# A sixth tile of the first MLP product let into PSUM during the second inverse stage, and another order for the first token tile

## Chip, cores, metric

One core of a Trainium2 chip. The metric is the device time of one execution in microseconds (us); runs of one kernel mostly agree within 0.3%. TensorE does the matmuls; DVE is VectorE, ACT is ScalarE; PSUM is the memory of eight banks into which TensorE writes. The kernel before takes 133.91 us (median of 4, 133.81 to 134.03).

## The reference, cut to what matters

```python
x = A_x                                   # (1, 2048, 512), bf16
h = x + irfft2(rfft2(layernorm(x)) * W)   # spectral mixing
n = layernorm(layernorm(h))
u = gelu(einsum("bsd,sf->bdf", n, w1) + b1)      # first MLP product, over tokens: 2048 -> 1376
y = einsum("bdf,fs->bds", u, w2) + b2            # second MLP product: 1376 -> 2048
out = h + y.transpose(0, 2, 1)
```

The MLP mixes tokens. So the first product needs every token: its 11 output tiles of 128 features (the last has 96) each accumulate over 16 token tiles.

## The kernel before

The kernel records operations with their tiles, and a small list scheduler written in Python fixes, before anything runs, each engine's order and each PSUM bank. On the chip every engine goes through its list in order; semaphores hold an instruction until what it needs is there. A *unit* is one use of a bank; the unit's class has a limit of how many may be open at once, and a unit that is not `early` opens only when all of its inputs are scheduled.

The names of the prediction stand for these operations, for each token tile n:

```python
for s2 in range(NS2):                       # 16 token tiles
    unit = PsumUnit("g2", 1)
    for par in (1, 0):
        for pq in range(2):
            mm(f"g2_{s2}_{par}{pq}", ...)   # "g2": 4 matmuls, 256 columns
    act(f"eo_{s2}", EO[:, s2, :], ...)      # "eo": PSUM -> bf16, frees g2's bank
    unit = PsumUnit("g3", 1)
    mm(f"g3_{s2}", ...)                     # "g3": 1 matmul, 512 columns
    dve(f"tl_{s2}", ...)                    # "tl", "th": the two halves of TT
    dve(f"th_{s2}", ...)
    dve(f"h_{s2}", ...)                     # "h": the residual stream H, frees g3's bank
    act(f"q_{s2}", ...Square...accum=V2)    # "q": sum of squares
    act(f"r2_{s2}", ...)                    # "r": inverse root
    dve(f"hh_{s2}", ...)                    # "hh": normalised token tile HH
    for t in range(5):
        mm1(t, s2)                          # "mm1 t/n": 512 columns, one per open tile
# ... cut ...
for t in range(5, NFT):
    for s2 in range(NS2):
        mm1(t, s2)                          # the other six tiles
# ... gelu of each tile, then the second product: 16 x 11 matmuls, 16 x "fin", 16 stores
```

Of the eight banks five are kept by mm1 tiles 0 to 4 late in this stage. The rest serve g2 and g3.

## Time and profile before

| | before |
|---|---|
| time, median | 133.91 us |
| span of the profiled run | 132.2 us |
| first g2 matmul starts | 39.84 us |
| last matmul ends | 128.86 us |
| TensorE issue idle between these two, holes over 0.025 us | 2.26 us |

The last row is counted from the starts of TensorE's matmuls; a *hole* is what a start comes later than the spacing of two matmuls allows. The prediction shows how, with the lines that carry it.

### The profile page before, as it was taken

How to read it: one execution, taken by the hardware profiler on the slowest of the kernel's cores; microseconds unless marked ns; L12 is line 12 of the kernel's file. 1: busy time of each engine (PE TensorE's matmuls, PEld its weight loads, DVE VectorE, ACT ScalarE, POOL GpSimd, SP SyncE). 2: the span in 40 equal slices, each digit the busy share in tenths (PEclk: the TensorE clock that was granted, in tenths of full speed). 3: DMA queues.
4: the chain of work that ended last, by engine and by line, in shares of the span. 5: the costliest groups of instructions: out<-in, count | busy, mean ns of one | idle time of the engine just before them, and what ended most of it. 6: DMA issues, size and time to landing. Idle time of an engine off the chain costs nothing.

```text
span 132.2 us, 2004 instructions
## 1 busy us (share of the span) xinstructions
PE 123.3 (93%) x773; PEld 73.2 (55%) x773; DVE 70.5 (53%) x133; ACT 62.7 (47%) x144; POOL 10.7 (8%) x30
## 2 busy tenths in 40 slices
PE   6799989999979799999989999999999999999990
PEld 2145656878757455444334444456666666666650
DVE  0599978999973999999950000000332422423322
ACT  4299966789867999966699222222000000000000
POOL 0089900003000000000000000000000000000000
PEclk9999999999999999999999999999999999999998
DMA  3999999999999999980000000000112112121121
GB/s 110 340 401 388 303 291 295 297 215 332 394 418 416 410 413 413 386 208 31 0 0 0 0 0 0 0 5 0 40 40 79 40 40 79 45 75 44 40 79 40
DMA packets 16920, 22.16 MB, mean 168 GB/s; under 512 B 2736, under 2 KB 12720, under 8 KB 16912
## 3 DMA queue, kind: packets, MB, share of 16 engines
q1 hardware_dynamic: 16624, 21.52, 48.6%
q10 hardware_dynamic: 288, 0.52, 1.4%
q8 instruction: 6, 0.10, 0.3%
q14 instruction: 2, 0.02, 0.0%
HBM read 19.95 MB, written 2.10 MB: 167 GB/s over the span
## 4 chain that ended last, share of the span: by engine, by line
PE 60%; ACT 16%; DVE 16%; DMA 3%; issue 3%
PE ps L553 60%; ACT JK L571 5%; ACT Y L571 4%; DVE H L903 4%; DVE V L828 3%; DMA X<-in_A_x_dram 3%; ACT EO L571 3%; DVE HH L908 2%; ACT rs L571 2%; DVE TT L894 2%; DVE TT L896 2%; ACT r L571 2%; ACT FS L571 1%; DVE Y L744 1%; ACT PQ L571 1%
## 5 line engine op out<-in xcount | busy, mean ns | idle before, releaser
L553 PE MATMUL ps<-HH,W 128*128 128x512 bf16 (+1 forms) x176 | 41.0, 379 | 1.3 <-DVE HH L908 1.1
L553 PE MATMUL ps<-GT,W 128*128 128x512 bf16 (+1 forms) x176 | 38.2, 379 | 0.0
L933 DVE SCALAR_TENSOR_TENSOR OUT<-ps,B2f,H 128x512 bf16<-128x512 f32 x16 | 12.0, 750 | 48.7 <-PE ps L553 48.7
L553 PEld LDWEIGHTS ps<-GT,W 128*128 128x128 bf16 (+1 forms) x176 | 25.5, 145 | 12.6
L553 PEld LDWEIGHTS ps<-HH,W 128*128 128x128 bf16 (+1 forms) x176 | 17.1, 100 | 22.1 <-DVE HH L908 2.2
L828 DVE TENSOR_TENSOR V<-ps,W 128x2048 bf16<-128x2048 f32 (+1 forms) x8 | 15.7, 2017 | 0.4 <-PE ps L553 0.2
L571 ACT ACTIVATE GT<-ps,B1f 128x512 bf16<-128x512 f32 (+1 forms) x11 | 7.1, 688 | 14.6 <-PE ps L553 14.6
L571 ACT ACTIVATE JK<-H,nm 128x512 bf16<-128x512 bf16 x16 | 11.6, 726 | 3.4 <-DVE H L903 3.2
L682 DVE BATCH_NORM_STATS2 st<-X 128x6 f32<-128x512 bf16 x15 | 9.8, 665 | 3.6 <-DMA X<-in_A_x_dram 3.6
L903 DVE TENSOR_TENSOR H<-ps,TT 128x512 bf16<-128x512 f32 x16 | 10.9, 681 | 0.0
L571 ACT ACTIVATE PQ<-ps 128x512 bf16<-128x512 f32 (+1 forms) x16 | 9.1, 591 | 3.7 <-PE ps L553 3.6
L553 PE MATMUL ps<-EM,V 128*128 128x128 bf16 x128 | 9.6, 220 | 0.4 <-ACT PQ L571 0.3
L571 ACT ACTIVATE EO<-ps 128x512 bf16<-128x512 f32 x16 | 9.3, 600 | 0.9 <-PE ps L553 0.9
L648 PE MATMUL ps<-ZT 128*128 128x512 bf16 x21 | 7.6, 481 | 2.1 <-DVE ZT L591 1.2
L553 PE MATMUL ps<-FS,X 128*128 128x256 bf16 x64 | 8.6, 274 | 0.8 <-ACT FS L571 0.5
L571 ACT ACTIVATE CS<-ps 128x512 bf16<-128x512 f32 (+1 forms) x16 | 8.4, 577 | 1.6 <-PE ps L553 1.6
L553 PEld LDWEIGHTS ps<-EM,V 128*128 128x128 bf16 x128 | 7.8, 98 | 2.5 <-issue 1.3
L553 PE MATMUL ps<-EM,PQ 128*128 128x256 bf16 x64 | 8.6, 273 | 0.5 <-ACT PQ L571 0.5
L553 PE MATMUL ps<-EM,Y 128*128 128x256 bf16 x64 | 8.6, 273 | 0.4 <-DVE Y L744 0.4
L571 ACT ACTIVATE Y<-ps 128x512 bf16<-128x512 f32 (+1 forms) x15 | 7.9, 566 | 0.2 <-PE ps L553 0.2
L660 POOL TENSOR_SCALAR FS<-FP,rs 128x256 bf16<-128x256 bf16 x8 | 7.4, 937 | 6.7 <-ACT rs L571 6.4
L894 DVE TENSOR_TENSOR TT<-ps,X 128x256 f32<-128x256 f32 x16 | 6.7, 416 | 2.1 <-PE ps L553 2.1
(38 smaller groups left out, 77.9 us busy)
## 6 DMA issues: line engine op xcount, KB each, us to landing
W<-in_B_w_dram SPq DMA_DIRECT2D x8, 688.0 KB, 9.6
W<-in_B_w_dram SPq DMA_DIRECT2D x10, 512.0 KB, 17.0
out_dram<-OUT SPq DMA_DIRECT2D x16, 128.0 KB, 1.7
W<-in_A_w_r_dram SPq DMA_DIRECT2D x4, 257.0 KB, 5.2
W<-in_A_w_i_dram SPq DMA_DIRECT2D x4, 257.0 KB, 5.7
X<-in_A_x_dram SPq DMA_DIRECT2D x4, 256.0 KB, 5.0
X<-in_A_x_dram SPq DMA_DIRECT2D x2, 512.0 KB, 6.6
W<-in_A_w_r_dram SPq DMA_DIRECT2D x4, 192.8 KB, 4.5
```

What stands on the lines that cost most here:

```text
L553: return K.op(name, "pe", lambda eng, bank: eng.matmul(outf(bank), lhsT, rhs, start=start, stop=stop), ins=ins or [lhsT, rhs], occ=occ, la ...
L571: return eng.activation(dst, s, func, **kw)
L648: return K.op(name, "pe", lambda eng, bank: eng.matmul(ps[:, bank, :], ZT[:, 0:NP], ZT[:, :], start=True, stop=True), ins=[ZT[:, :]], occ= ...
L660: dve(f"fs_{i}", lambda eng, bank: eng.tensor_scalar(FS[:, i, :, :], FP[:, i, :, :], rs, None, op0=ALU.mult), [FP[:, i, :, :], rs], [FS[:, ...
L682: dve(f"bn_{i}", lambda eng, bank, i=i, x=x: eng.bn_stats(ST[:, i, 0:6], x), [x], [ST[:, i, 0:6]], 512, prio=25)
L744: dve(name, lambda eng, bank: eng.tensor_copy(dst, src(bank)), [], [dst], n, unit=unit, prio=28, last=last)
L828: return eng.tensor_tensor(vout, s, win, ALU.mult)
L894: dve(f"tl_{s2}", lambda eng, bank, tt=tt, xl=xl: eng.tensor_tensor(tt[:, 0, :], ps[:, bank, 256:512], xl, ALU.add), [xl], [tt[:, 0, :]], ...
L896: dve(f"th_{s2}", lambda eng, bank, tt=tt, xh=xh: eng.tensor_tensor(tt[:, 1, :], xh, ps[:, bank, 256:512], ALU.subtract), [xh], [tt[:, 1, ...
L903: return eng.tensor_tensor(hs.rearrange("p (h d) -> p h d", h=2), e, tt[:, :, :], ALU.add)
L908: dve(f"hh_{s2}", lambda eng, bank, s2=s2, hs=hs: eng.tensor_scalar(HH[:, s2, :], hs, NM[:, s2:s2 + 1], R2[:, s2:s2 + 1], op0=ALU.add, op1 ...
L933: dve(f"fin{s2}", lambda eng, bank, dst=dst, bia=bia, hs=hs: eng.scalar_tensor_tensor(dst, ps[:, bank, :], bia, hs, op0=ALU.add, op1=ALU.add),
```

## The change

It means to fill TensorE's idle time in the second inverse stage. Three things are meant: tile 5 and tile 6 of mm1 may take a bank as soon as one is free; DVE and ACT finish token 0 ahead of the next tokens, so that mm1 can begin sooner; and g2 of tokens 0 to 7 has a limit of its own, so that g2 of later tokens may open beside it.

```diff
-    "dve": """... fs_13 fs_14 fs_15 ys_12 ys_14""",
+    "dve": """... fs_13 fs_14 fs_15 ys_12 ys_14
+        tl_0 th_0 h_0 tl_1 th_1 h_1 hh_0""",
-    "act": """... ys_11 ys_13 yh_150 yh_151""",
+    "act": """... ys_11 ys_13 yh_150 yh_151
+        eo_0 eo_1 eo_2 eo_3 eo_4 q_0 r2_0 eo_5""",
+MM1B_FROM = {5: 54000.0, 6: 62000.0}
-    K = Builder(nc, {..., "g2": 2, "g3": 2, "mm1": 5, "mm1b": 6, "mm2": 8})
+    K = Builder(nc, {..., "g2a": 2, "g2": 2, "g3": 2, "mm1": 5, "mm1b": 6, "mm2": 8})
-            w1units[t] = PsumUnit("mm1" if t < 5 else "mm1b", 1, early=t < 5)
+            w1units[t] = PsumUnit("mm1" if t < 5 else "mm1b", 1, early=t < 7)
         mm(f"mm1_{t}_{s2}", ...,
-           s2 == 0, s2 == NS2 - 1, s2 == 0, 2 if t < 5 else 1, 512)
+           s2 == 0, s2 == NS2 - 1, s2 == 0, 2 if t < 5 else 1 if t < 6 else 0.5, 512, nb=MM1B_FROM.get(t, 0.0))
     for s2 in range(NS2):
-        unit = PsumUnit("g2", 1)
+        unit = PsumUnit("g2a" if s2 < 8 else "g2", 1)
```

(`mm` hands `nb` on as an earliest start, in ns of the scheduler's own clock.) No operation is added or taken away.

More of the change, by code (lines that the diff above doesn't have):

```diff
@@ L500 @@
     "dve": """bn_0 ag_0 bn_1 ag_1 bn_2 bn_4 ag_2 bn_5 ag_4 bn_6 ag_5 bn_7 ag_6 bn_8 ag_7 bn_9 ag_8 bn_10 ag_9 bn_11 ag_10 bn_12 ag_11
-        fs_9 ag_12 bn_13 fs_11 ag_13 bn_14 bn_15 ag_14 ag_15 fs_13 fs_14 fs_15 ys_12 ys_14""",
+        fs_9 ag_12 bn_13 fs_11 ag_13 bn_14 bn_15 ag_14 ag_15 fs_13 fs_14 fs_15 ys_12 ys_14
+        tl_0 th_0 h_0 tl_1 th_1 h_1 hh_0""",
     "act": """rs_0 fs_0 rs_1 s1_3 s2_3 rs_2 rs_3 fs_3 rs_4 ys_0 rs_5 ys_1 ys_3 rs_6 ys_2 fs_7 rs_8 ys_4 ys_5 rs_9 ys_7 rs_11 ys_6 ys_8
-        rs_13 ys_9 ys_10 rs_14 ys_11 ys_13 yh_150 yh_151""",
+        rs_13 ys_9 ys_10 rs_14 ys_11 ys_13 yh_150 yh_151
+        eo_0 eo_1 eo_2 eo_3 eo_4 q_0 r2_0 eo_5""",
     "pool": """fs_1 bv_3 fs_2 fs_4 fs_5 fs_6 fs_8 fs_10 fs_12""",
@@ L520, in build_kernel @@
     es.__enter__()
-    K = Builder(nc, {"f1": 7, "f2": 2, "x": 2, "g1": 2, "g2": 2, "g3": 2, "mm1": 5, "mm1b": 6, "mm2": 8})
+    K = Builder(nc, {"f1": 7, "f2": 2, "x": 2, "g1": 2, "g2a": 2, "g2": 2, "g3": 2, "mm1": 5, "mm1b": 6, "mm2": 8})
     K.forced = {e: FRONT[e].split() for e in ("dve", "act", "pool")}
@@ L545, in dma, with mm @@
                     rate=rate, occ=1000.0 if stream == "pool" else 640.0 if rate < DMA_RATE else 460.0, not_before=not_before, stall=stall)
-    def mm(name, outf, lhsT, rhs, unit, start, stop, first, prio, n, ins=None, half=False, after=()):
+    def mm(name, outf, lhsT, rhs, unit, start, stop, first, prio, n, ins=None, half=False, after=(), nb=0.0):
         occ = n / 2.4 + 3.0
@@ L553, in mm @@
         return K.op(name, "pe", lambda eng, bank: eng.matmul(outf(bank), lhsT, rhs, start=start, stop=stop),
-                    ins=ins or [lhsT, rhs], occ=occ, lat=n / 2.4 + 220.0, unit=unit, pw=True, first=first, prio=prio, after=after)
+                    ins=ins or [lhsT, rhs], occ=occ, lat=n / 2.4 + 220.0, unit=unit, pw=True, first=first, prio=prio, after=after, not_before=nb)
     def act(name, dst, src, func, n, ins=(), outs=None, unit=None, prio=0, last=True, psum=True, bias=None, scale=None, accum=None):
```

## The prediction

> **Names.** The second stage runs, for each of 16 token tiles n: four 256-column matmuls PQ to PSUM ("g2"), an ACT copy to EO ("eo"), one 512-column matmul ("g3"), three DVE ops (two halves of TT, called tl and th, then H, called h), on ACT the sum of squares (written to JK, "q") and its inverse root ("r"), and on DVE the normalised HH ("hh"). Each hh n releases one matmul of 512 columns per open tile t of the first MLP product ("mm1 t/n", 11 tiles). After that come the rest of mm1, the gelus, and 176 matmuls of the second product.
>
> **What bounds the kernel now.** I read the chain in order of time first. Its end:
> ```profile
> 66.30 0.34 DVE TT L896
> 66.64 0.02 issue
> 66.66 0.69 DVE H L903
> 67.35 0.33 DVE HH L908
> 67.68 0.05 issue
> 67.73 61.15 PE ps L553 x282
> 128.88 0.03 issue
> 128.90 0.75 DVE OUT L933
> ```
> From 67.73 us to 128.88 TensorE issues 282 matmuls back to back. 282 is 176 + 176 less the 70 mm1 matmuls done by then. There is no hole in them, so before that only two things can shorten the run: less TensorE work, or less TensorE idle time. The change removes no matmul. So the question is how much TensorE idles before 67.73 us, and how much of that stays. Before 39.84 us, where g2 begins, both programs have the same instructions in the same order.
>
> I measure idle time at TensorE's issue and not from its busy share, because the records overlap:
> ```profile
> 55.59 2.32 PE L553 MATMUL ps<-HH,W 128*128 128x512 bf16 x10
> ```
> Ten matmuls take 2.32 us, with 0.38 for the last one: (2.32 - 0.38)/9 = 0.216 us each, and likewise 0.109 for 256 columns (13 in 1.59 us). Then I took the TensorE timeline, start by start, and counted what each start comes later than the one before plus 0.216 or 0.109. The largest hole, and one of the late ones:
> ```profile
> 44.64 0.38 PE L553 MATMUL ps<-EO,IF 128*128 128x512 bf16 x1
> 45.88 0.38 PE L553 MATMUL ps<-HH,W 128*128 128x512 bf16 x1 [0.86 <-DVE HH L908]
> ...
> 64.23 1.87 PE L553 MATMUL ps<-HH,W 128*128 128x512 bf16 x7
> 66.35 2.84 PE L553 MATMUL ps<-HH,W 128*128 128x512 bf16 x11 [0.26 <-DVE HH L908]
> ```
> The first is 45.88 - 44.64 - 0.22 = 1.02 us of lost issue. All seven holes: 1.02 ahead of mm1 0/0 (waits for hh 0), 0.19 ahead of 0/1 (hh 1), 0.08 and 0.06 ahead of g3 5 and 8 (eo), 0.20, 0.42 and 0.29 ahead of 0/12, 0/13 and 0/14 (their hh). Sum 2.26 us. That is all that the change can win: 1.7% of 133.87.
>
> Why the holes: DVE. By windows,
> ```profile
> 50.00:55.00 5.00, 5.00 (x33) 2.73 (x31) 4.84 (x13) 5.00 (x15) 0.00 (x0) 1.00 1.02 415
> 55.00:60.00 5.00, 5.00 (x25) 2.29 (x24) 4.98 (x13) 3.53 (x10) 0.00 (x0) 1.00 0.86 223
> 60.00:65.00 5.00, 4.96 (x24) 2.10 (x23) 5.00 (x14) 3.54 (x10) 0.00 (x0) 1.00 0.05 14
> ```
> (columns: stretch, length, then busy PE, weight loads, DVE, ACT, POOL, clock, DMA share, GB/s) DVE is full. Spaced start to start in its timeline, tl and th take 0.33 each, h 0.60, hh 0.33: 1.59 us a token. TensorE needs 5 x 0.216 + 0.216 (g3) = 1.30. So TensorE catches up with DVE and from token 12 on waits for each hh.
>
> **What the Trainium skill says.** "TensorE: Matmul & The Clock Gate", section "Back-to-back issue gap", gives N/2.4 + 2.5 ns for a warm isolated matmul, 216 ns at 512 columns: the trace agrees with 0.216. The same section has about 131 ns for streams with weight loads; this trace, which has one load per matmul, doesn't show that. "Perfetto Trace Analysis", section "Identifying the Most-Contended Engine", warns that matmul busy time is no good measure of headroom: agreed, the windows say 5.00 of 5.00 where smaller holes sit between starts. "PSUM — Partial Sum Buffer", section "The four PSUM rules", has one matmul output in one of 8 banks, so a tile that is open holds a bank: here five tiles leave three banks to g3. "VectorE: DVE Perf Modes", section "The DRAIN you can't avoid", says that a Vector op reading what the one just before wrote still needs a semaphore; th then h directly takes 0.45 us start to start here (66.21 to 66.66), against 0.33 with an op between.
>
> **The change, part by part.** It adds and removes nothing; it moves. I took the new order on each engine with its waits and walked it with the spacings of the trace before: ACT eo to eo 0.49, eo to q 0.48, q to eo 0.71, eo to r 0.47, r to next 0.19, q to r direct 0.85; a released op starts 0.03 to 0.05 after the record it waits for, mm1 0.06 after hh (0.15 where it also waits for a load).
>
> (1) *First tile ahead.* h 0 now follows th 0 directly: 42.03 + 0.45 = 42.48, not 42.69. eo 5 no longer precedes q 0, which starts 0.48 after eo 4's 42.72: 43.20 instead of 43.81. Then eo 6 at 43.91, r 0 at 44.38, ended 44.67, hh 0 at 44.71 to 45.12, mm1 0/0 at 45.27 (was 45.88). In front of it TensorE now has g2 9 as well (up to 45.08), since tokens 8 and up have their own limit of two open g2 banks. The hole of 1.02 becomes 0.19.
>
> (2) *A new wait.* mm1 0/0, 1/0, 2/0 go at 45.27, 45.49, 45.71. Next stands g3 4, in the bank that g2 7 used, so it waits for eo 7. ACT: r 0 44.38, eo 5 44.57, q 1 45.05, eo 7 45.76 to 46.36; g3 4 at 46.41, where 45.92 was possible: 0.49 lost. This is the greatest loss that I find in the new order. It displaces the holes of 0.19 and 0.08 of before.
>
> (3) *Tokens 1 to 11.* On from there: mm1 0/1 at 47.29 and g2 11 at 48.36 start without a wait; mm1 0/2 waits for hh 2 (r 2 ends 48.37, hh 2 48.41 to 48.82), 0.07 lost; g2 13 waits for h 5, 0.03 lost. After it, eo, h and hh are each ready before TensorE comes to them (mm1 0/5 at 55.21 with hh 5 ended 53.45; 0/9 at 60.18 with hh 9 ended 59.88; 0/10 at 61.91 with hh 10 at 61.47).
>
> (4) *Tile 5 as filler.* h 11 frees its bank at 61.1, and ten matmuls of tile 5 stand between there and mm1 0/14: 2.16 us that ran after 67.73 before. The late waits against them: mm1 0/12 at 65.15 with hh 12 ended 64.95 (plus 0.15: just in time), 0/13 at 66.88 with 66.68, 0/14 at 68.39 with 68.06, 0/15 at 69.69 with 69.36. So 0.20 + 0.42 + 0.29 = 0.91 goes. Tile 6, though let in, stands wholly behind tile 5's last, so it fills nothing. DVE ends its last hh 0.4 us later than before (69.36 against 68.97), which costs nothing as long as filler covers it.
>
> (5) *Loads.* The last part of the first weights lands at 46.3 us, before any use in either order; the second weights by 62.1. No transfer is moved.
>
> Sum: idle after 0.19 + 0.49 + 0.07 + 0.03 = 0.78 us against 2.26; gain 1.48. Everything from mm1 0/15 on keeps its work and, but for bank numbers, its order. 133.87 - 1.48 = 132.39 us, 1.1% less.
>
> **Rivals.** (a) *DVE stays the bound and takes the gain back.* For it: DVE full for 10 us, and it ends later by my walk. Then some holes of 0.91 reappear at 0/12 to 0/15, where my slack is 0.05 to 0.3 us; with half of them back, 132.8; with nothing gained, 133.9. Against it: filler needs no hh that isn't there, and DVE needs only the last hh 1.3 us after TensorE has 0/14. (b) *All holes close:* 131.6. It needs g3 4 not to wait; ACT's order says it will. (c) *The wait on eo 7 is dearer.* ACT is full until 55 us and orders eo 5 behind r 0, so everything behind it is tight; if q 1 or eo 7 slips by 0.5 us, 132.9. (d) *Slower:* a sixth tile leaves two banks to g3, so a late h delays g3, then DVE (I find one such: tl 14 waits 0.3 us for g3 14). To lose over 1.5 us it would have to happen at every token; the order puts it in the last four only.
>
> **Range and chances.** The three runs before lie within 0.22 us. My walk's error is the sum of some forty small spacings on ACT and the slack at 0/12; I give 0.5 us either way, the lower end short of all holes closed. 131.9 to 132.9. Over 2% faster needs 131.2, below the floor of 131.6, so only an effect that I don't see: 3%. Over 2% slower would need new waits of 4 us: 1%.
>
> **What would show it.** In the profile after: mm1 0/0 near 45.3 us; a TensorE hole near 46 us released by ACT's EO, about 0.5 us; no hole after 52 us; the unbroken run to the end counting more than 282 matmuls, and starting earlier. Wrong would be: holes on HH after 60 us (rival a), or the same start of g3 4 but a hole near 1 us (rival c).

## The result, and the profile after

132.43 us (median of 4, 132.34 to 132.51) against 133.91. The ratio is 0.9889, with a 95% interval of 0.9872 to 0.9906. Ratios here are the mean time of one kernel's fast runs over that of the other's fast runs of the same rounds, so not quite the ratio of the medians. That is 1.1% faster, 1.48 us by the medians.

The first trace of the changed kernel holds 763 of its 773 matmul records (and all 773 weight loads), so its chain looks broken where nothing waits. Its end, piece by piece in order of time (start us, length us, what):

```profile
46.30 7.90 PE ps L556 x47
54.20 0.05 issue
54.26 10.74 PE ps L556 x49
65.00 0.05 issue
65.05 10.74 PE ps L556 x49
```

Each break takes the length of one matmul, 0.216 us from start to start in excess, and the next comes 49 records on: a lost record and not a wait. The same kernel was profiled once more in the experiments below (after_again), with all 773 records, and the views of the changed kernel from here on are from that trace. The end of its chain:

```profile
45.89 0.50 ACT EO L574
46.39 0.05 issue
46.43 80.95 PE ps L556 x385
127.39 0.02 issue
127.41 0.75 DVE OUT L936
```

Before, the unbroken run began at 67.73 us with 282 matmuls, behind 13 us of DVE's TT, H and HH. Now it begins at 46.43 us with 385 matmuls, and DVE is no longer in the chain between there and the end. (Two holes of 0.08 and 0.03 us lie inside this run; the overlap of the records hides them from the chain.) TensorE's timeline around the largest hole that is left, and late in the stage (start, length, then what; in brackets the idle time):

```profile
44.44 0.82 PE L556 MATMUL ps<-EM,PQ 128*128 128x256 bf16 x6
45.30 0.81 PE L556 MATMUL ps<-HH,W 128*128 128x512 bf16 x3
46.43 0.39 PE L556 MATMUL ps<-EO,IF 128*128 128x512 bf16 x1 [0.33 <-ACT EO L574]
46.66 0.60 PE L556 MATMUL ps<-EM,PQ 128*128 128x256 bf16 x4
...
64.96 0.38 PE L556 MATMUL ps<-EO,IF 128*128 128x512 bf16 x1
65.18 10.09 PE L556 MATMUL ps<-HH,W 128*128 128x512 bf16 x46
```

mm1 0/0 begins at 45.30 us (was 45.88). The hole ahead of g3 4 is 46.43 - 45.30 - 3 x 0.216 = 0.48 us of issue (0.49 unrounded); the bracket says 0.33 because it counts from the modelled end of the matmul before. From 65.18 us, where mm1 0/12 starts, 46 matmuls run without a break up to 75 us, where the view was cut, through the places where mm1 waited for HH before. By windows (columns as in the prediction):

```profile
50.00:55.00 5.00, 5.00 (x32) 2.81 (x31) 5.00 (x14) 5.00 (x15) 0.00 (x0) 1.00 1.03 418
55.00:60.00 5.00, 5.00 (x25) 2.23 (x23) 5.00 (x14) 3.53 (x10) 0.00 (x0) 1.00 0.84 215
60.00:65.00 5.00, 5.00 (x25) 2.23 (x23) 4.74 (x13) 3.18 (x10) 0.00 (x0) 1.00 0.04 13
```

DVE, the third of the engines, is as full as before up to 60 us, and busy 4.74 of 5.00 us after that, where it waits for TensorE's g3 14. It has not become faster; TensorE only has something else to do. Holes of the two kernels, from the starts:

| hole ahead of | waits for | before | after |
|---|---|---|---|
| mm1 0/0 | hh 0 | 1.02 | 0.20 |
| g3 4 | eo 7 | - | 0.49 |
| mm1 0/1 | hh 1 | 0.19 | - |
| g3 5, g3 8 | eo 8, eo 13 | 0.08, 0.06 | - |
| mm1 0/2 | hh 2 | - | 0.08 |
| g2 13 | h 5 | - | 0.03 |
| mm1 0/12, 0/13, 0/14 | hh 12, 13, 14 | 0.20, 0.42, 0.29 | - |
| sum | | 2.26 | 0.79 |

### The profile page after: what moved, and what is told of

Same layout as the page of the kernel before. It is cut to its first block, busy times and chain, and to the rows that moved or that the text cites. A ratio compares the mean times of both kernels' runs of the same rounds, so it can differ in the third digit from the quotient of the medians.

```text
span 130.6 us, 1996 instructions
## 1 busy us (share of the span) xinstructions
PE 122.4 (94%) x763; PEld 73.6 (56%) x773; DVE 70.7 (54%) x133; ACT 62.5 (48%) x144; POOL 10.8 (8%) x30
## 4 chain that ended last, share of the span: by engine, by line
PE 75%; ACT 12%; DVE 6%; DMA 3%; issue 2%
PE ps L556 75%; ACT Y L574 4%; DVE V L831 3%; DMA X<-in_A_x_dram 3%; ACT rs L574 2%; ACT JK L574 2%; ACT EO L574 2%; ACT FS L574 1%; DVE Y L747 1%; ACT PQ L574 1%; DVE OUT L936 1%; DVE st L685 1%; DVE FS L663 0%; PE ps L651 0%; ACT r L574 0%
## 5 line engine op out<-in xcount | busy, mean ns | idle before, releaser
L556 PE MATMUL ps<-HH,W 128*128 128x512 bf16 (+1 forms) x173 | 40.1, 379 | 0.4 <-DVE TT L899 0.2
```

Source lines behind the costliest of these rows:

```text
L556: return K.op(name, "pe", lambda eng, bank: eng.matmul(outf(bank), lhsT, rhs, start=start, stop=stop), ins=ins or [lhsT, rhs], occ=occ, la ...
```

## The experiments

Each kernel differs from the one before or the changed one by the edit shown. The start of g2 moves between profiled runs by up to half a microsecond (39.69 to 40.18 us in these traces) with nothing of the change ahead of it; so the table also gives the stretch from the first g2 start to the end of the last matmul, which is free of that. Lost records are counted as one matmul each, so they don't show up as holes. The medians of the kernel before differ between groups of rounds (133.91 to 134.00).

| run | time, median (runs) | before, same rounds | ratio, 95% | g2 start to last matmul |
|---|---|---|---|---|
| the kernel before | 133.91 (4) | | | 89.02 |
| front_only | 133.83 (5) | 133.95 | 0.9986, 0.9974 to 0.9999 | 88.92 |
| fill_only | 133.01 (5) | 133.95 | 0.9924, 0.9911 to 0.9938 | 88.10 |
| front_g2shared | 132.54 (4) | 133.95 | 0.9889, 0.9876 to 0.9903 | 87.63 |
| before_tl_half | 133.30 (5) | 133.95 | 0.9947, 0.9934 to 0.9959 | 88.38 |
| after_again | 132.44 (4) | 134.00 | 0.9883, 0.9866 to 0.9899 | 87.51 |
| eo7_first | 132.57 (4) | 134.00 | 0.9900, 0.9886 to 0.9915 | 87.65 |
| after_q_half | 132.16 (4) | 134.00 | 0.9864, 0.9849 to 0.9879 | 87.21 |
| minimal | 132.58 (4) | 133.98 | 0.9893, 0.9876 to 0.9909 | 87.51 |

All results are right but those of before_tl_half and after_q_half. The comparison with the reference calls before_tl_half wrong; after_q_half alters only a normalisation factor and stays within the tolerance.

### front_only: the order without the filler

```diff
-            w1units[t] = PsumUnit("mm1" if t < 5 else "mm1b", 1, early=t < 7)
+            w1units[t] = PsumUnit("mm1" if t < 5 else "mm1b", 1, early=t < 5)
-MM1B_FROM = {5: 54000.0, 6: 62000.0}
+MM1B_FROM = {}
```
(from the changed kernel; the priority goes back too)

> The change without its filler: the new order on DVE and ACT and the separate limit for g2 stay, tile 5 starts after the second stage as before. My theory: DVE sets the pace from token 9 on (1.59 us a token against TensorE's 1.30), so what TensorE wins at tokens 0 to 4 it waits out again at tokens 10 to 14. Walking the order with the spacings of the trace: early holes 0.78 us, late holes back and larger, about 0.03, 0.29, 0.39, 0.41, 0.30 ahead of mm1 0/10 to 0/14, sum 2.2 against 2.3 before; time about 133.8, gain 0.1 us. Rival, the parts simply add: early holes fall from 1.34 to 0.78 and the late 0.91 stay, so a gain of about 0.56 and 133.35. Rival, the order alone does it all: 132.4.

133.83 us, 0.1 us faster; over the stretch also 0.10. The early holes are those of the changed kernel (0.19, 0.49, 0.08), 0.60 less than before. The late ones have grown: 0.28, 0.37, 0.42, 0.29 ahead of mm1 0/11 to 0/14, 1.35 in place of 0.91. TensorE's timeline there:

```profile
63.88 0.59 PE L556 MATMUL ps<-HH,W 128*128 128x512 bf16 x2
64.68 1.02 PE L556 MATMUL ps<-HH,W 128*128 128x512 bf16 x4 [0.20 <-DVE HH L911]
66.17 2.20 PE L556 MATMUL ps<-HH,W 128*128 128x512 bf16 x8 [0.47 <-DVE HH L911]
```

(mm1 0/12 starts at 64.68, 0/13 at 66.17. The record of mm1 4/12, which ran between, is lost, so the second bracket holds its 0.216 too.) So TensorE, arriving earlier, waited longer for the same DVE. The rival "the parts add" (133.35) lies clearly outside; so does "the order does it all".

### fill_only: the filler without the order

```diff
-            w1units[t] = PsumUnit("mm1" if t < 5 else "mm1b", 1, early=t < 5)
+            w1units[t] = PsumUnit("mm1" if t < 5 else "mm1b", 1, early=t < 7)
```
(from the kernel before, with the two start times)

> The kernel before with tile 5 (and 6) let in early and nothing else: DVE and ACT orders and the g2 limit are those of before. My theory: the late holes ahead of mm1 0/12 to 0/14 go, the early ones (1.02, 0.19, 0.08, 0.06) stay; idle about 1.4 us, time about 133.05, gain 0.86 us. Together with the front alone (0.1) that is less than the whole 1.48: the two need each other. Rival, DVE takes the gain back: 133.6 or more, holes on HH after 60 us. Rival, the filler does it all: 132.4.

133.01 us, 0.94 less by the medians, 0.92 over the stretch. Its holes are the four early ones of before (1.02, 0.20, 0.08, 0.06, sum 1.36); none is left after 53.1 us. The early one in TensorE's timeline:

```profile
44.32 0.60 PE L554 MATMUL ps<-EM,PQ 128*128 128x256 bf16 x4
45.99 0.38 PE L554 MATMUL ps<-HH,W 128*128 128x512 bf16 x1 [1.07 <-DVE HH L909]
```

(The g3 4 record between these two is lost; with it the hole is 1.02.) Alone, the parts give 0.10 and 0.92 over the stretch, 1.02 in all; together 1.51. The difference of 0.5 us is most of the early gain, which only counts when the later wait on DVE is filled.

### front_g2shared: the whole change with one limit for all g2

```diff
-        unit = PsumUnit("g2a" if s2 < 8 else "g2", 1)
+        unit = PsumUnit("g2", 1)
```
(from the changed kernel, with `"g2a": 2` gone)

> The whole change, but g2 of all tokens under one limit of two open banks as before. My theory: g2 9 no longer stands in front of mm1 0/0, so its hole is about 0.62 in place of 0.19, and g2 9 then waits for eo 7, about 0.27 in place of 0.49; idle 0.92 against 0.78, time about 132.55, 0.14 us slower than the change. Rival, the limit is what closes the first hole: about 132.85 (0.43 lost, the wait on eo 7 unchanged).

132.54 us; holes 0.63 ahead of mm1 0/0, 0.27 ahead of g2 9 (eo 7), 0.03, sum 0.93. The stretch is 0.12 us longer than the changed kernel's. The two lay in different rounds, so the times (ratios of 0.9889 and 0.9883 to the kernel before) do not separate them, but the holes do, as expected: the own limit lets g2 9 run ahead into the wait for hh 0, and half of what it wins there is paid back at eo 7.

### before_tl_half: less DVE work a token

```diff
+        tn = 128 if s2 >= 4 else 256
-        ... eng.tensor_tensor(tt[:, 0, :], ps[:, bank, 256:512], xl, ALU.add)
+        ... eng.tensor_tensor(tt[:, 0, 0:tn], ps[:, bank, 256:256 + tn], xl[:, 0:tn], ALU.add)
```
(from the kernel before; wrong result)

> The kernel before with tl over 128 columns in place of 256 for tokens 4 to 15; wrong result on purpose, order and waits the same. It tests what the late holes are made of. My theory, DVE's pace: some 0.13 us less a token, so mm1 0/12 and 0/13 wait no more and 0/14 about 0.24; time about 133.3, 0.6 us less than before. Rival, the late holes are the latency of ACT's q and r behind h: no change, 133.9.

133.30 us, 0.65 less. The end of its chain in order of time:

```profile
64.13 0.33 DVE TT L897
64.46 0.20 DVE TT L895
64.66 0.60 DVE H L904
65.26 0.32 DVE HH L909
65.58 0.34 DVE TT L897
65.92 0.02 issue
65.95 0.69 DVE H L904
66.64 0.33 DVE HH L909
66.97 0.05 issue
67.02 8.82 PE ps L553 x40
```

tl takes 0.20 us in place of 0.33, a token's four DVE operations 1.45 in place of 1.59. The holes ahead of mm1 0/12 and 0/13 are gone and 0/14 waits 0.26. Less DVE time, with q and r untouched, removes the late waits: they are made of DVE's pace. The rival (latency of q and r) would have left 133.9.

### after_again, eo7_first, after_q_half: what holds the rest

> The changed kernel as it is, on the same chip and rounds as the two below: 132.4 us, holes of 0.19, 0.49, 0.07, 0.03.

132.44 us, holes of 0.20, 0.49, 0.08 and 0.03: the result repeats in other rounds.

eo7_first puts eo 7 ahead of q 1, to take the new wait away:

```diff
-        eo_0 eo_1 eo_2 eo_3 eo_4 q_0 r2_0 eo_5""",
+        eo_0 eo_1 eo_2 eo_3 eo_4 q_0 eo_6 r2_0 eo_5 eo_7 q_1""",
```

> The changed kernel with eo 7 placed ahead of q 1 on ACT, so that the wait of g3 4 for eo 7 goes. My theory: ACT is full there and the banks are all held, so the wait only changes its name: g3 4 waits no more, but g2 10 waits for h 2 (0.30) and mm1 0/1 for hh 1, which q 1 now delays (0.40); idle 0.96 against 0.78, time about 132.6, 0.2 us slower than the change. Rival, the order of these two is a plain slip of the change: 0.49 gained, 131.9.

132.57 us against 132.44 on the same chip: 0.13 slower by the medians, 0.14 over the stretch. TensorE's timeline:

```profile
45.62 0.81 PE L556 MATMUL ps<-HH,W 128*128 128x512 bf16 x3
46.27 0.38 PE L556 MATMUL ps<-EO,IF 128*128 128x512 bf16 x1
46.80 0.61 PE L556 MATMUL ps<-EM,PQ 128*128 128x256 bf16 x4
47.24 0.39 PE L556 MATMUL ps<-HH,W 128*128 128x512 bf16 x1
47.88 0.82 PE L556 MATMUL ps<-HH,W 128*128 128x512 bf16 x3 [0.24 <-DVE HH L911]
```

g3 4 (46.27) follows the three mm1 matmuls with no hole, and the loss has gone to g2 10 (0.31, h 2's bank) and mm1 0/1 (0.42, hh 1 behind the later q 1). So the wait on eo 7 is not a plain slip of these two; other orders were not tried.

after_q_half leaves the order and takes ACT's load down:

```diff
+        qn = 256 if s2 < 7 else 512
-        act(f"q_{s2}", junk()[:, :], hs, ACT.Square, 512, ...)
+        act(f"q_{s2}", junk()[:, 0:qn], H[:, s2, 0:qn], ACT.Square, 512, ...)
```

> The changed kernel with q over 256 of 512 columns for tokens 0 to 6 (0.21 us less ACT time for each); wrong result on purpose, order and waits the same. If ACT's load holds what is left, the wait on eo 7 falls from 0.49 to about 0.18 and about 0.1 comes back ahead of g2 10 (h 2); idle about 0.5 against 0.78, time about 132.15, 0.27 us faster. Rival, what is left is fixed latency of the chain from g2 to hh: less than 0.1 us faster.

132.16 us, 0.28 less than the changed kernel. On ACT, q now takes 0.41 us from start to start in place of 0.62. TensorE's timeline:

```profile
45.24 0.81 PE L556 MATMUL ps<-HH,W 128*128 128x512 bf16 x3
46.06 0.39 PE L556 MATMUL ps<-EO,IF 128*128 128x512 bf16 x1
```

The hole at eo 7 is 0.18 (46.06 - 45.24 - 3 x 0.216, unrounded), the others 0.14, 0.13 (g2 10) and 0.06, sum 0.51 against 0.79. So less ACT work takes 0.31 of the 0.49 us away, of which 0.13 comes back at g2 10. What holds the remaining 0.51 us was not tested.

### minimal: three parts of the change taken out

```diff
-        rs_13 ys_9 ... yh_150 yh_151
-        eo_0 eo_1 eo_2 eo_3 eo_4 q_0 r2_0 eo_5""",
+        rs_13 ys_9 ... yh_150 yh_151""",
-MM1B_FROM = {5: 54000.0, 6: 62000.0}
+MM1B_FROM = {}
-    ... early=t < 7)
+    ... early=t < 6)
```

> The changed kernel without the three parts that look idle in its order: the tail of the ACT list, the two start times, and tile 6. Without the start times and tile 6 the program comes out the same, instruction for instruction; without the ACT tail only eo 5 and eo 6 change places, and with them two banks. My theory: those parts do nothing, 132.4 us as the change. Rival, the place of eo 5 matters: mm1 2/0 then waits for eo 6 in its place, and some tenths are lost, 132.6 or more.

132.58 us (132.42 to 132.78), ratio 0.9893, whose interval overlaps that of the changed kernel (0.9883); the holes are the same (0.20, 0.49, 0.08) and the stretch is 87.51 us, equal to the changed kernel's to the hundredth. In the profiled run all that it is longer by lies ahead of g2, which began at 40.13 us; for the other runs that stays open. So what the change does is done by the DVE order, g2's own limit and tile 5 alone. The start times and tile 6 leave the scheduled order as it is, instruction for instruction; the ACT tail only makes eo 5 and eo 6 change places.

## Why the prediction was right

*What bounds it.* The prediction put all that could be won into TensorE's idle time ahead of 67.73 us, 2.26 us. From kernel to kernel the stretch changes as the sum of holes does, within 0.07 us (before to after: 1.51 against 1.47; fill_only: 0.92 against 0.90; before_tl_half, with 1.62 us of holes: 0.64 against 0.64). Since every kernel has the same matmuls, this checks the count and not the cause: it says that their spacing stayed the same. One reading was too broad. "Why the holes: DVE" holds for the late holes; but the chain of the kernel before runs over ACT (EO, JK, r) from 42.23 us on, and over DVE only from 54.99, and between 45 and 50 us ACT is busy 5.00 of 5.00 us. The walk had ACT's waits in it, so the sum did not suffer. Nor did TensorE wait for each hh from token 12 on: mm1 0/15 had no hole before the change either.

*Step 1, the first tile ahead.* Foreseen: hh 0 at 44.71 to 45.12 us, mm1 0/0 at 45.27, a hole of 0.19. Measured: 44.74 to 45.15, 45.30, 0.20.

*Step 2, the new wait.* Foreseen: g3 4 at 46.41 us, 0.49 lost to eo 7. Measured: 46.43, 0.49. eo7_first and after_q_half show its nature, which the prediction had only argued: ACT is full and the banks are held, so the one other order that was tried moves the wait, and less ACT work shortens it.

*Step 3, tokens 1 to 11.* Foreseen 0.07 and 0.03, measured 0.08 and 0.03.

*Step 4, the filler.* Foreseen: mm1 0/12 at 65.15, 0/13 at 66.88, 0/14 at 68.39, 0/15 at 69.69, no wait. Measured: 65.18, 66.91, 68.42, 69.71, no wait. The slack at 0/12 was as thin as said: hh 12 ended at 65.00. Tile 6 was said to fill nothing; it starts at 71.87, behind tile 5's last.

*Step 5, loads.* No hole waits for a load that is late, in either kernel: the last part of the first weights lands at 46.33 us before and 46.05 after, and mm1 0/12, which uses it, starts at 64.86 and 65.18. But mm1 0/0 and 0/12 also have a load's semaphore to check. They start 0.15 us after their hh (45.15 to 45.30 after the change), where mm1 0/2 starts 0.06 after its own (48.86 to 48.92). So about half of the 0.20 us that is left ahead of mm1 0/0 is not hh 0. That it is the second wait was not tested.

*The sum.* 1.48 us foreseen, 1.48 measured by the medians; 132.39 against 132.43. That it agrees to the hundredth is luck: over the stretch the gain is 1.51, and by the medians of after_again's rounds 1.56.

*The rivals.* (a) DVE taking the gain back did not come about, but front_only shows that it does without the filler: 0.60 us won early, 0.44 of it given back late. Whoever had judged the order by itself would have thrown it away. The prediction credited each part with its own holes and did not see this; since both parts are in the change, its sum was not touched. (b) All holes closing did not happen; (c) the dearer wait, and (d), did not either: tl 14 waits for g3 14, and nothing of it reaches TensorE.

The method's reach should be kept in view: the forecast was close because the order on each engine is fixed, each duration was in the trace before, and no clock or transfer changed.

## What to carry to other kernels

Where several engines pass tokens along in a fixed order, count the idle time at the issue of the engine that runs to the end; that sum is the ceiling of any reordering of that stage which leaves the engine's work as it is, and a walk through the new order with measured spacings tells how much of it stays. A gain early in such a stage is lost again when a slower engine sets the pace later, unless independent work is there to fill that later wait; so test such parts together as well as alone. Look in the scheduled order for knobs that change nothing: here the start times, the ACT list and one of two added tiles.

## What the Trainium skill lacked or had wrong

- "TensorE: Matmul & The Clock Gate", section "Back-to-back issue gap": for streams of weight load and matmul it has about 131 ns at 512 columns. In every trace here such pairs go at 0.216 us, its value for an isolated matmul; e.g. ten in 2.32 us with 0.38 for the last.
- "VectorE: DVE Perf Modes", section "The DRAIN you can't avoid", says of eight copies with a semaphore after each that it costs nothing extra there. It does not say whether each copy waited for the one before. Here h right behind the th whose result it waits for starts 0.45 us after it (66.21 to 66.66 us in the kernel before), against 0.33 with another op between or with an op that does not depend: 0.12 us more.
- "Perfetto Trace Analysis", section "Tensor Engine Instruction (MATMUL, LD_WEIGHTS)", says that a matmul's end is estimated. That section does not say that records of matmuls can be lost: the first trace of the changed kernel has 763 matmuls of 773, and each lost one looks like a hole of 0.216 us; the weight loads, 773, tell it.
